# Strided x transposed by DMA instead of by TensorE, from the fifth batch on

## Chip, cores and metric

The kernel runs on one core of a Trainium2 chip. The metric is the device time of one launch in microseconds. One launch is profiled as well, and the views below come from that execution. TensorE is called PE, VectorE DVE, ScalarE ACT, GpSimd POOL and SyncE SP, as in the profile.

## What is computed

Sparse attention, and a two-layer network with an ELU on its output:

```
# q, k, v: (8 batches, 8 heads, 576 rows, 64)
rel  = pos[:, None] - pos[None, :]
local   = (rel >= 0) & (rel < 32)                    # heads 0 to 3
strided = (rel >= 0) & (key % 32 == query % 32)      # heads 4 to 7
attn = softmax(where(mask, q @ k.T / 8, -1e9)); y = attn @ v
x = y.transpose(0, 2, 1, 3).reshape(4608, 512)
h = x @ w_in                                         # 512 -> 2048
out = where(h > 0, h, exp(min(h, 0)) - 1) @ w_out    # 2048 -> 512
```

## The kernel before

**Attention.** Heads are taken in pairs, two local pairs (l0, l1) and two strided pairs (s0, s1) for each batch, all in bf16. For strided heads rows are regrouped by their remainder modulo 32, so that each of five groups of 108 or 126 rows needs only keys of the same group. q and k come from HBM in their natural layout, rows on partitions, into a ring of three tiles for each kind (`nat`), by software DMA that POOL issues (L191 to L219). From batch 3 on they are transposed to features on partitions by DMA transposes that SP issues (`transpose_batch`, L222).

A pair then runs in pieces: scores on PE (`scores_all`, L466) into the two banks of `pair_a` and two single banks; exp on ACT and mask on DVE; two value products on PE (`av`, L552), each followed on DVE by a reciprocal and the division into the tile x (L579, L580); and `x_out` (L595), which brings x to features on partitions in `xT`. For local pairs from batch 4 on, `x_out` is a DMA transpose from x right into `xT` (L599). For strided pairs PE transposes five groups into a PSUM bank (L607), and ACT copies them into `xT` in the order of the rows (L614, L616), since the groups interleave.

**MLP.** Tokens go in nine chunks of 512. In chunk nb, slot s = 0 to 15 issues one group of four matmuls of the first product (`moe_in`, L664; operands c = 0 to 3 of `xT`, of which c = 2 and 3 are the strided pairs s0 and s1), its ELU (`moe_act`, ACT L690, DVE L697 and L699) and one group of four of the second product (`moe_out`, L713). Every fourth such group ends an output block of 128 rows: ACT copies it to `o_sb` (L718) and SP stores it (L720).

**Order.** Nothing is scheduled by a planner: the program order on each engine is written out. While chunk nb runs, batch nb + 1 goes through attention, its pieces hung into half-slots: half-slot 2s comes ahead of `moe_in` of slot s, 2s + 1 behind it. A row of `TIMES` gives the half-slot where each of the four pairs begins and `PIECES` the offsets of its pieces. From batch 4 on local pairs come first. The first group of chunk nb + 1 needs the columns of batch nb + 1, so `x_out` of the last pair, at half-slot 31, is close to its reader.

SP's queue holds, in program order, the stores, the DMA transposes of q and k of batch nb + 2 and those of x; each waits at the head of the queue for its inputs. PSUM banks are handed out in rings; in these chunks two single banks (`ring`) serve the scores' last blocks, the value products and the strided transposes in turn.

The pieces of batch 4 and later, before:

```
PIECES = (-2, -1, 0, 2, 3, 5, 7, 0)
((2, 8, 15, 22), 0, PIECES)     # where the four pairs begin
# scores at +0, value products at +3 and +5 (+4 for the first pair)
(at[6] + (b > 1 and pr.strided) + (b >= LATE), pr.x_out)
```

Of the kernel before, what the change touches and what calls it, by code (L numbers as in the profile page):

```python
# [14 lines left out]
ACT = mybir.ActivationFunctionType  # L15
# [14 lines left out]
C_ORDER = (2, 3, 0, 1)  # L30


PIECES = (-2, -1, 0, 2, 3, 5, 7, 0)
TIMES = (
    None,
    None,
    ((4, 10, 15, 21), 0, (-3, -2, 0, 2, 4, 6, 9, 2)),
    ((2, 9, 15, 22), 0, (-2, -1, 0, 2, 3, 5, 8, 0)),
    ((2, 8, 15, 22), 0, PIECES),
)  # L40


# [23 lines left out]
def kernel(  # L66
# [66 lines left out]
    def bf16_bank():  # L133
        return rings["ring"].next().bitcast(BF16)
# [17 lines left out]
    def several(n, name, *shape):  # L152
        return [consts.tile([128, *shape], BF16, tag=f"{name}{i}", name=f"{name}{i}")
                for i in range(n)]

    nat = {(n, kind): several(3, f"{n}_{kind}", w * D)
           for n in "qk" for kind, w in (("str", 20), ("loc", 4 * L_RUN))}

# [10 lines left out]
    BY_DMA = 3  # L171

    WHOLE = 2

    FAR = 1
    RAW = 1
# [42 lines left out]
                out=t[0:64, a, 4],  # L219
                in_=src[name][b, 2 * a:2 * a + 2, 512:576].rearrange("h p d -> p h d"))  # L220

    def transpose_batch(b, local):  # L222

        def strided():
            for name, to in (("q", qT), ("k", kT)):
                nc.sync.dma_start_transpose(out=to["str"][b % 2],
                                            in_=nat[name, "str"][b % 3])

        if BY_DMA <= b <= LATE and local < 2:
            strided()  # L230
        if b >= EARLY and local:
            for name, to, o in (("q", qT, 0), ("k", kT, 32)):
                for a in range(2):
                    nc.sync.dma_start_transpose(
                        out=to["loc"][b % 2][:, a, o:o + 640].rearrange(
                            "p (i r) -> p i r", r=128),
                        in_=nat[name, "loc"][b % 3][:, 640 * a:640 * a + 640])
        if b > LATE:
            strided()

    def load_batch(b):
        for name in "qkv":
# [9 lines left out]
    def clear_nat(i, names="kq", heads=slice(0, 4)):  # L252

        for name in names:
            t = nat[name, "str"][i].rearrange("p (h x) -> p h x", h=4)
            nc.vector.memset(t[96:128, heads], 0.0)
# [6 lines left out]
    def clear_v(i, engine=nc.vector):  # L263
# [8 lines left out]
             for n in "q"}  # L272
# [2 lines left out]
    nc.scalar.activation(warm, ones[0:1, 0:1], ACT.Exp)  # L275
    nc.scalar.activation(rden.rearrange("p b s h r g -> p (b s h r g)"),
                         ones.to_broadcast([128, B * 48]), ACT.Copy)
    clear_nat(0)
    for i in range(2):
        nc.vector.memset(kT["str"][i][:, :, 126:128], 0.0)  # L280
# [70 lines left out]
    class Pair:  # L351
# [200 lines left out]
        def av(self, u):  # L552
            blocks = self.blocks(u)
            nk, nq = blocks[0][4:]
            b0 = blocks[0][1]
            n = len(blocks) // 2
            av = rings["ring"].next()[:, 0:6 * (D + 1)].rearrange(
                "q (p g d) -> q p g d", p=2, g=3)
            apart = self.strided and self.b == RAW
            vt = raw[RAW] if apart else (v_str if self.strided else v_loc)[self.b % 3]  # L560
            for p, blk, bank, i, _, _ in blocks:

                if self.b >= WHOLE:
                    pr, o, top = self.pr_all, self.probs[p, blk], 1152
                else:
                    pr, o, top = self.pr[u], (bank * n + i) * nq, 2 * n * nq
                m = 128 if o + 128 <= top else nq
                to = av[0:m, p, blk - b0, :]
                nc.tensor.matmul(to[:, 0:D] if apart else to, lhsT=pr[0:nk, o:o + m],  # L569
                                 rhs=vt[0:nk, 2 * self.hp + p, blk, :],  # L570
                                 start=True, stop=True)
                if apart:
                    nc.tensor.matmul(to[:, D:], lhsT=pr[0:nk, o:o + m],
                                     rhs=ones[0:nk, :], start=True, stop=True)
            if self.x is None:
                self.x = p_x.tile([128, 6, 2, D], BF16, tag=f"x_{self.kind}",
                                  name=f"x_{self.kind}")
            r = rden[0:nq, self.b, int(self.strided), self.hp, :, b0:b0 + n]
            nc.vector.reciprocal(r, av[0:nq, :, 0:n, D])  # L579
            nc.vector.tensor_tensor(  # L580
                self.x[0:nq, b0:b0 + n].rearrange("q g p d -> q p g d"),
                av[0:nq, :, 0:n, 0:D],
                r.unsqueeze(3).to_broadcast([nq, 2, n, D]),
                op=ALU.mult)

        def step(self, what):
# [5 lines left out]
            else:  # L592
                getattr(self, {"x": "x_out"}.get(what, what))()

        def x_out(self):  # L595
            c = 2 * int(self.strided) + self.hp
            dst = xT[:, c, self.b * S:(self.b + 1) * S]
            if self.b >= LATE and not self.strided:
                nc.sync.dma_start_transpose(  # L599
                    out=dst.rearrange("d (i q) -> d i q", i=6),  # L600
                    in_=self.x[0:LB].rearrange("q i p d -> q (i p d)"))
                return
            xt = bf16_bank()
            if self.strided:
                for g in range(5):
                    n = G_ROWS[g]
                    nc.tensor.transpose(  # L607
                        xt[:, 126 * g:126 * g + n],
                        self.x[0:n, g].rearrange("q p d -> q (p d)"),
                        identity[0:n, 0:n])  # L610
                rows = dst.rearrange("d (t r) -> d t r", r=STRIDE)
                groups = xt[:, 0:630].rearrange("d (g q) -> d g q", g=5)
                copy = self.copy("x", False)
                copy(rows[:, :, 0:30].rearrange("d t (r g) -> d t r g", g=5),  # L614
                     groups[:, :, 0:108].rearrange("d g (t r) -> d t r g", r=6))
                copy(rows[:, :, 30:32],  # L616
                     groups[:, 0:2, 108:126].rearrange("d g t -> d t g"))
            else:
                for i in range(6):
                    nc.tensor.transpose(  # L620
                        xt[:, LB * i:LB * (i + 1)],
                        self.x[0:LB, i].rearrange("q p d -> q (p d)"),
                        identity[0:LB, 0:LB])
                self.copy("x", self.b > 1)(dst, xt[:, 0:S])
# [10 lines left out]
    def attention(b, start, pitch, at):  # L635

        gaps = {}
        pairs = [Pair(b, s, hp) for s in (b < LATE, b >= LATE) for hp in range(2)]
        begin = [start + pitch * i for i in range(4)] if pitch else start
        if b >= LATE:  # L640
            gaps[begin[0]] = [pairs[3].halo]
        for i, pr in enumerate(pairs):
            for off, piece in ((at[0], pr.t_q), (at[1], pr.t_k),
                               (at[7], lambda pr=pr: pr.v_in(0)),
                               (at[7] + (b > 1), lambda pr=pr: pr.v_in(1)),
                               (at[2], lambda pr=pr: pr.scores(0)),
                               (at[3] if b < WHOLE else at[2] + (b < LATE),
                                lambda pr=pr: pr.scores(1)),
                               (at[4], lambda pr=pr: pr.av(0)),
                               (at[5] - (b >= LATE and i == 0),  # L650
                                lambda pr=pr: pr.av(1)),
                               (at[6] + (b > 1 and pr.strided) + (b >= LATE), pr.x_out), (at[5] - 2, pr.halo if b < LATE else lambda: None)):
                gaps.setdefault(begin[i] + off, []).append(piece)
        return gaps


# [145 lines left out]
    for nb in range(n_chunks + 1):  # L802
# [14 lines left out]
        for s in range(MC):  # L817
            if nb == 0 and s == 11:
                share([pair_a], b_halves, singles[3:], singles[:3])
            if s == (9 if nb + 2 > LATE else 6) and nb > 0 and nb + 2 < B:  # L820
                transpose_batch(nb + 2, int(nb + 2 >= LATE))
            if s == 13 and nb + 2 == EARLY:
                transpose_batch(nb + 2, 2)
            run(gaps, (2 * s,) if s else range(-10, 1))
            late = LATE <= nb + 1 and s + 1 < MC
            if nb < n_chunks:
                moe_in(nb, s)
            if nb < n_chunks and not late:
                moe_act(nb, s)
            run(gaps, (2 * s + 1,) if s + 1 < MC else range(2 * s + 1, 1000))  # L830
            if nb < n_chunks and late:
                moe_act(nb, s)
            if nb == B and s == 4:
                range_flag(row_ok16)
            for chunk, i in outs(nb, s):
                moe_out(chunk, i)
# [165 lines left out]
```

## Time and profile before

| | |
|---|---|
| Runs | 321.51, 318.53, 321.12 us (median 321.12) |
| Profiled execution | 318.57 us, span 316.8 us |
| Busy in the span | PE 95%, DVE 77%, ACT 55%, POOL 43% |
| Mean granted PE clock | 0.996 |
| DMA | 36.33 MB, mean 115 GB/s |
| Strided transposes of x on PE (L607) | 80, of which 40 in batches 4 to 7 |
| DMA transposes issued by SP | 10 + 10 local q and k, 5 + 5 strided q and k, 8 local x |

In the page a group is a line, engine, operation and tiles, with its count, busy time and mean. In the timeline the first column is the start in us from the start of the span, the second the length; a bracket gives the idle time ahead of the instruction and what ended it. The busy time of PE is modelled, and matmuls overlap. PEld is the loading of weights. SPq is SP's instruction queue: its DMA rows are the time of issuing, and the time to landing stands in the DMA issue rows.

### The profile page before, as it was taken

How to read it: one execution, taken by the hardware profiler on the slowest of the kernel's cores; microseconds unless marked ns; L12 is line 12 of the kernel's file. 1: busy time of each engine (PE TensorE's matmuls, PEld its weight loads, DVE VectorE, ACT ScalarE, POOL GpSimd, SP SyncE). 2: the span in 40 equal slices, each digit the busy share in tenths (PEclk: the TensorE clock that was granted, in tenths of full speed). 3: DMA queues.
4: the chain of work that ended last, by engine and by line, in shares of the span. 5: the costliest groups of instructions: out<-in, count | busy, mean ns of one | idle time of the engine just before them, and what ended most of it. 6: DMA issues, size and time to landing. Idle time of an engine off the chain costs nothing.

```text
span 316.8 us, 6114 instructions
## 1 busy us (share of the span) xinstructions
PE 299.8 (95%) x2240; PEld 149.1 (47%) x2240; DVE 242.6 (77%) x544; ACT 172.9 (55%) x335; POOL 137.5 (43%) x213
## 2 busy tenths in 40 slices
PE   1778989999999999999999999999999999999994
PEld 0454545545444554445444544454445444444443
DVE  7787797887889998987898788878897666766610
ACT  3577886777355645565546555655565444343411
POOL 9859526959959859958585810000000000000000
PEclk9999999999999999999999999999999999999998
DMA  6999999999999999999999992580210000101012
GB/s 108 163 179 157 167 207 126 156 124 183 139 125 167 157 187 138 99 163 154 177 163 117 163 175 61 88 156 35 68 35 35 34 33 35 66 34 36 33 68 73
DMA packets 108970, 36.33 MB, mean 115 GB/s; under 512 B 87357, under 2 KB 104453, under 8 KB 108933
## 3 DMA queue, kind: packets, MB, share of 16 engines
q0 software_dynamic: 71632, 18.10, 65.0%
q1 hardware_dynamic: 37301, 17.77, 29.1%
q8 instruction: 19, 0.31, 0.4%
q14 instruction: 18, 0.15, 0.1%
HBM read 36.70 MB, written 9.44 MB: 146 GB/s over the span
## 4 chain that ended last, share of the span: by engine, by line
PE 84%; DMA 6%; DVE 3%; POOL 2%; ACT 2%; issue 1%; POOLq 0%; ACTq 0%
PE single L713 39%; PE half L664 28%; PE single L664 9%; PE single L569 3%; DMA q_str<-in_q_dram 3%; PE pair_a L479 2%; DMA v_raw<-in_v_dram 2%; DMA k_str<-in_k_dram 2%; PE single L607 1%; ACT e_sb L690 1%; POOL k_str L191 1%; PE single L397 1%; DVE g_sb L699 1%; PE single L383 1%; DVE x_l L580 1%
## 5 line engine op out<-in xcount | busy, mean ns | idle before, releaser
L713 PE MATMUL single<-w_out_sb,g_sb 128*128 128x512 bf16 (+1 forms) x592 | 145.9, 373 | 0.0
L664 PE MATMUL half<-xT,w_in_sb 128*128 128x512 bf16 x436 | 112.6, 379 | 0.9 <-DVE g_sb L699 0.9
L690 ACT ACTIVATE e_sb<-half 128x512 f32<-128x512 f32 x109 | 65.3, 600 | 70.9 <-PE half L664 67.9
L697 DVE TENSOR_SCALAR e_sb<-e_sb 128x512 bf16<-128x512 f32 x140 | 62.5, 446 | 34.9 <-ACT e_sb L690 34.4
L713 PEld LDWEIGHTS <-g_sb 128*128 128x128 bf16 x592 | 54.8, 98 | 56.6
L664 PEld LDWEIGHTS <-w_in_sb 128*128 128x128 bf16 x576 | 52.4, 98 | 57.0 <-issue 1.3
L699 DVE TENSOR_TENSOR g_sb<-e_sb,half 128x512 bf16<-128x512 bf16 x106 | 72.9, 688 | 3.7
L664 PE MATMUL single<-xT,w_in_sb 128*128 128x512 bf16 x140 | 36.5, 379 | 0.0
L690 ACT ACTIVATE e_sb<-single 128x512 f32<-128x512 f32 x35 | 21.1, 602 | 24.4 <-PE single L664 22.3
L718 ACT COPY o_sb<-single 128x512 f32<-128x512 f32 (+1 forms) x37 | 21.2, 574 | 17.5 <-PE single L713 16.7
L485 ACT ACTIVATE pr<-pair_a 126x936 bf16<-126x936 f32 (+1 forms) x24 | 23.1, 961 | 12.4 <-PE single L479 11.9
L569 PEld LDWEIGHTS <-pr 128*128 128x128 bf16 (+3 forms) x352 | 20.0, 101 | 13.7 <-issue 1.3
L699 DVE TENSOR_TENSOR g_sb<-e_sb,single 128x512 bf16<-128x512 bf16 x34 | 23.4, 688 | 1.2
L191 POOL DMA_DIRECT2D k_str<-in_k_dram x32 | 21.1, 698 | 6.8 <-issue 2.6
L191 POOL DMA_DIRECT2D v_raw<-in_v_dram x32 | 20.7, 683 | 5.0 <-DVE v_str L436 3.7
L191 POOL DMA_DIRECT2D q_str<-in_q_dram x28 | 17.4, 641 | 4.1 <-DMA w_out_sb<-in_moe_w_out_dram 2.3
L580 DVE TENSOR_TENSOR x_l<-single,rden 96x384 bf16<-96x384 f32 x32 | 17.7, 554 | 1.1
L580 DVE TENSOR_TENSOR x_s<-single,rden 126x256 bf16<-126x256 f32 (+1 forms) x32 | 15.7, 491 | 1.1
L214 POOL DMA_DIRECT2D k_loc<-in_k_dram x20 | 15.3, 795 | 2.5 <-issue 1.5
L214 POOL DMA_DIRECT2D q_loc<-in_q_dram x20 | 15.8, 813 | 0.7 <-DMA k_str<-in_k_dram 0.7
L579 DVE RECIPROCAL rden<-single 96x6 f32<-96x6 f32 (+2 forms) x64 | 11.8, 185 | 2.0 <-PE single L569 1.6
L569 PE MATMUL single<-v_loc,pr 128*128 128x65 bf16 x192 | 11.6, 195 | 0.8 <-ACT v_loc L444 0.3
(115 smaller groups left out, 249.6 us busy)
## 6 DMA issues: line engine op xcount, KB each, us to landing
out_dram<-o_sb SPq DMA_DIRECT2D x35, 256.0 KB, 3.6
v_loc<-in_v_dram POOLq DMA_DIRECT2D x8, 288.0 KB, 8.2
k_str<-in_k_dram POOLq DMA_DIRECT2D x32, 67.5 KB, 5.0
v_raw<-in_v_dram POOLq DMA_DIRECT2D x32, 67.5 KB, 4.8
w_in_sb<-in_moe_w_in_dram POOLq DMA_DIRECT2D x4, 512.0 KB, 8.2
w_out_sb<-in_moe_w_out_dram POOLq DMA_DIRECT2D x4, 512.0 KB, 13.6
q_str<-in_q_dram POOLq DMA_DIRECT2D x28, 67.5 KB, 7.5
q_loc<-in_q_dram POOLq DMA_DIRECT2D x20, 64.0 KB, 5.2
```

The costliest lines, as they stand in the source:

```text
L191: engine.dma_start(out=t[0:108, h].rearrange("p g d -> p (g d)"), in_=rows[h, :, 0:30, :].rearrange("t (r g) d -> t r (g d)", g=5))
L214: nc.gpsimd.dma_start(out=t[:, h // 2, 0:4, h % 2], in_=src[name][b, h, 0:512].rearrange("(i p) d -> p i d", p=128))
L485: nc.scalar.activation(both, sc[0:nk, :, 0:w], ACT.Exp, scale=scale)
L569: nc.tensor.matmul(to[:, 0:D] if apart else to, lhsT=pr[0:nk, o:o + m], rhs=vt[0:nk, 2 * self.hp + p, blk, :], start=True, stop=True)
L579: nc.vector.reciprocal(r, av[0:nq, :, 0:n, D])
L580: nc.vector.tensor_tensor(self.x[0:nq, b0:b0 + n].rearrange("q g p d -> q p g d"), av[0:nq, :, 0:n, 0:D], r.unsqueeze(3).to_broadcast([nq, ...
L664: nc.tensor.matmul(hps, lhsT=w_in_sb[:, c, m * 128:(m + 1) * 128], rhs=xT[:, c, nb * N_TILE:(nb + 1) * N_TILE], start=start, stop=stop)
L690: nc.scalar.activation(e_sb, hps, ACT.Exp)
L697: nc.vector.tensor_scalar(e1_sb, e_sb, scalar1=1.0, scalar2=1.0, op0=ALU.min, op1=ALU.subtract)
L699: nc.vector.tensor_tensor(g_of[nb][:, m, :], e1_sb, hps, op=ALU.max)
L713: nc.tensor.matmul(ops, lhsT=g_of[nb][:, m, kk * 128:(kk + 1) * 128], rhs=w_out_sb[:, m, cols], start=(m == 0), stop=(m == MC - 1))
L718: nc.scalar.copy(o_sb, ops)
```

## The change

From batch 4 on (`X_DMA`), the x of a strided pair is transposed by a DMA that SP issues, one half-slot after the second value product. It goes into the free part of the pair's own q tile (the strided q of that batch, already transposed), 640 of its 1280 columns for each pair. `x_out` copies from there on ACT; PE takes no part and no PSUM bank is used. `x_out` comes three half-slots later relative to the pair's beginning (`X_WAIT`), but never behind half-slot 31. The strided pairs begin at half-slots 14 and 20 instead of 15 and 22, so that s1's `x_out` stays at 31, s0's moves from 24 to 26, and the DMAs are issued at half-slots 20 and 26.

x of strided pairs lies in two tiles of its own, for all batches, whose last 32 partitions are set once at the start by two ACT instructions. `TURNS` spreads the transposes of q and k: for batches 5 and later local ones at slot 8, strided q at 11 and strided k at 14 (all six at slot 9 before); for batch 4 all at slot 6 as before, but local ones first.

```diff
+TURNS = ((13, 6, 6), (6, 6, 6), (8, 11, 14))
-    ((2, 8, 15, 22), 0, PIECES),
+    ((2, 8, 14, 20), 0, PIECES),
...
+    x_str = several(2, "x_s", 6, 2, D)
+    X_DMA = 4
+    X_ONE = LATE
+    X_WAIT = 3
...
-    def transpose_batch(b, local):
-        ...
+    def transpose_batch(b, s):
+        for what, at in zip(("loc", "str q", "str k"), TURNS[min(b - EARLY, 2)]):
+            if s != at:
+                continue
+            if what == "loc":
+                ...                       # four local transposes, as before
+            else:
+                name = what[-1]
+                nc.sync.dma_start_transpose(out=(qT if name == "q" else kT)["str"][b % 2],
                                             in_=nat[name, "str"][b % 3])
...
+    for i in range(2):
+        nc.scalar.activation(x_str[i][96:128].rearrange("q g p d -> q (g p d)"),
+                             ones[96:128].to_broadcast([32, 12 * D]), ACT.Copy)
...
-            if self.x is None:
+            if self.strided:
+                self.x = x_str[self.hp]
+            elif self.x is None:
...
+        def by_dma(self):
+            if self.strided:
+                return self.b >= X_DMA
+            return self.b >= LATE or self.b >= X_ONE and self.hp == 0
+        def x_dma(self):
+            if self.strided and self.by_dma():
+                free = nat["q", "str"][self.b % 3][:, 640 * self.hp:640 * self.hp + 640]
+                self.x_t = free.rearrange("d (g q) -> d g q", g=5)
+                nc.sync.dma_start_transpose(
+                    out=self.x_t,
+                    in_=self.x[:, 0:5].rearrange("q g p d -> q (g p d)"))
...
-            xt = bf16_bank()
+            if not self.by_dma():
+                xt = bf16_bank()
             if self.strided:
-                (five PE transposes; groups = xt ...)
+                if self.by_dma():
+                    groups = self.x_t
+                else:
+                    (five PE transposes; groups = xt ..., as before)
                 copy = self.copy("x", False)
...
-                               (at[6] + (b > 1 and pr.strided) + (b >= LATE), pr.x_out), ...):
-                gaps.setdefault(begin[i] + off, []).append(piece)
+                               (at[5] + 1, pr.x_dma),
+                               (at[6] + (b > 1 and pr.strided) + (b >= LATE)
+                                + X_WAIT * (pr.strided and pr.by_dma()), pr.x_out), ...):
+                gaps.setdefault(min(begin[i] + off, 31), []).append(piece)
...
-            if s == (9 if nb + 2 > LATE else 6) and nb > 0 and nb + 2 < B:
-                transpose_batch(nb + 2, int(nb + 2 >= LATE))
-            if s == 13 and nb + 2 == EARLY:
-                transpose_batch(nb + 2, 2)
+            if nb > 0 and nb + 2 < B:
+                if s in TURNS[min(nb + 2 - EARLY, 2)]:
+                    transpose_batch(nb + 2, s)
```

More of the change, by code (lines that the diff above doesn't have):

```diff
@@ L220, in load_local @@
                 in_=src[name][b, 2 * a:2 * a + 2, 512:576].rearrange("h p d -> p h d"))
-    def transpose_batch(b, local):
-        def strided():
-            for name, to in (("q", qT), ("k", kT)):
-                nc.sync.dma_start_transpose(out=to["str"][b % 2],
-                                            in_=nat[name, "str"][b % 3])
[L229 to L239, printed above, removed]
+    def transpose_batch(b, s):
[3 more added lines that the diff above has]
+            if what == "loc":
+                for name, to, o in (("q", qT, 0), ("k", kT, 32)):
+                    for a in range(2):
+                        nc.sync.dma_start_transpose(
+                            out=to["loc"][b % 2][:, a, o:o + 640].rearrange(
+                                "p (i r) -> p i r", r=128),
+                            in_=nat[name, "loc"][b % 3][:, 640 * a:640 * a + 640])
+            else:
+                name = what[-1]
+                nc.sync.dma_start_transpose(out=(qT if name == "q" else kT)["str"][b % 2],
+                                            in_=nat[name, "str"][b % 3])
     def load_batch(b):
@@ L593, in step @@
                 getattr(self, {"x": "x_out"}.get(what, what))()
+        def by_dma(self):
[6 more added lines that the diff above has]
+                self.x_t = free.rearrange("d (g q) -> d g q", g=5)
+                nc.sync.dma_start_transpose(
+                    out=self.x_t,
+                    in_=self.x[:, 0:5].rearrange("q g p d -> q (g p d)"))
         def x_out(self):
@@ L597, in x_out @@
             dst = xT[:, c, self.b * S:(self.b + 1) * S]
-            if self.b >= LATE and not self.strided:
+            if self.by_dma() and not self.strided:
                 nc.sync.dma_start_transpose(
@@ L602, in x_out @@
                 return
-            xt = bf16_bank()
+            if not self.by_dma():
+                xt = bf16_bank()
             if self.strided:
[L605 to L610, printed above, removed]
-                rows = dst.rearrange("d (t r) -> d t r", r=STRIDE)
-                groups = xt[:, 0:630].rearrange("d (g q) -> d g q", g=5)
+                rows = dst.rearrange("d (t r) -> d t r", r=STRIDE)
+                if self.by_dma():
+                    groups = self.x_t
+                else:
+                    for g in range(5):
+                        n = G_ROWS[g]
+                        nc.tensor.transpose(
+                            xt[:, 126 * g:126 * g + n],
+                            self.x[0:n, g].rearrange("q p d -> q (p d)"),
+                            identity[0:n, 0:n])
+                    groups = xt[:, 0:630].rearrange("d (g q) -> d g q", g=5)
                 copy = self.copy("x", False)
@@ L651, in attention @@
                                 lambda pr=pr: pr.av(1)),
-                               (at[6] + (b > 1 and pr.strided) + (b >= LATE), pr.x_out), (at[5] - 2, pr.halo if b < LATE else lambda: None)):
-                gaps.setdefault(begin[i] + off, []).append(piece)
+                               (at[5] + 1, pr.x_dma),
+                               (at[6] + (b > 1 and pr.strided) + (b >= LATE)
+                                + X_WAIT * (pr.strided and pr.by_dma()), pr.x_out), (at[5] - 2, pr.halo if b < LATE else lambda: None)):
+                gaps.setdefault(min(begin[i] + off, 31), []).append(piece)
         return gaps
```

## The prediction

> **What bounds the kernel now.** I read the page first: the engine totals and the chain that ended last.
>
> ```profile
> span 316.8 us, 6114 instructions
> PE 299.8 (95%) x2240; PEld 149.1 (47%) x2240; DVE 242.6 (77%) x544; ACT 172.9 (55%) x335; POOL 137.5 (43%) x213
> ...
> PE 84%; DMA 6%; DVE 3%; POOL 2%; ACT 2%; issue 1%; POOLq 0%; ACTq 0%
> ```
>
> TensorE is busy for 95% of the span and carries 84% of the chain. The average hides the stages, so I cut the span where a chunk of the first MLP product begins (the first L664 group after the pair of strided transposes). The windows are the four chunks, 3 to 6, in which batches 4 to 7 are worked on. The columns are window, length, then busy time and count of PE, PEld, DVE, ACT and POOL, granted clock, DMA share and GB/s.
>
> ```profile
> 119.46:150.74 31.28, 31.28 (x226) 15.14 (x225) 27.26 (x60) 17.41 (x35) 26.26 (x39) 1.00 1.55 137
> 150.74:182.41 31.67, 31.64 (x227) 15.22 (x226) 27.10 (x60) 17.78 (x37) 22.27 (x33) 1.00 1.56 155
> 182.41:213.86 31.45, 31.45 (x227) 15.23 (x226) 26.49 (x60) 17.67 (x37) 1.20 (x1) 1.00 0.77 120
> 213.86:245.00 31.14, 31.14 (x226) 15.14 (x225) 26.20 (x59) 17.36 (x37) 0.00 (x0) 1.00 0.15 44
> ```
>
> PE has no gap in any of them, at full clock. So a PE instruction that is taken out shortens the chunk by its own issue time, and a PE wait that is put in lengthens it by its whole length: nothing later gives it back. The last two columns make a second distinction: in chunks 3 and 4 the DMA engines are oversubscribed (1.55 counts overlapping packets), in chunk 5 only partly, in chunk 6 hardly.
>
> **What is removed.** Eight strided outputs (two in each of the four batches) lose five PE transposes each. Here is the second half of chunk 4 on PE, with the value products (L569) that the next part uses:
>
> ```profile
> 170.53 0.37 PE L569 MATMUL single<-v_str,pr 108*128 108x65 bf16 x6
> ...
> 175.77 0.29 PE L569 MATMUL single<-v_str,pr 126*128 126x65 bf16 x4
> ...
> 181.29 0.42 PE L607 MATMUL single<-identity,x_s 126*128 126x126 bf16 x5
> 181.55 1.03 PE L713 MATMUL single<-w_out_sb,g_sb 128*128 128x512 bf16 x4
> 182.41 1.03 PE L664 MATMUL half<-xT,w_in_sb 128*128 128x512 bf16 x4
> ```
>
> Matmuls overlap, so the price of a set is not 0.42 but the distance to the next start: 181.55 - 181.29 = 0.26 us. Eight sets: **-2.1 us**. By their busy time it would be 8 x 0.42 = 3.4 us, which I keep as the upper bound. This already caps the gain: 2.1 of 318.6 is 0.7%, and one per cent, 3.2 us, is about what a measurement of this kernel can tell from no change.
>
> **What is added, and where it can wait.** The second strided pair of a batch (s1) is the critical one. Its transposed x is the fourth operand (c = 3) of the first L664 group of the next chunk. Today PE transposes it just before and ScalarE copies it in time. After the change SP issues a transpose of 128x640 after the pair's last division, and ScalarE copies from the landing place at the same point of its program as now. I place it in chunk 4:
>
> ```profile
> 163.69 0.36 PE L569 MATMUL single<-v_loc,pr 128*128 128x65 bf16 x6
> 164.31 0.55 DVE L580 TENSOR_TENSOR x_l<-single,rden 96x384 bf16<-96x384 f32 x1
> ...
> 176.97 0.58 ACT L718 COPY o_sb<-single 128x512 f32<-128x512 f32 x1 [0.33 <-PE single L713]
> 177.83 0.60 ACT L690 ACTIVATE e_sb<-half 128x512 f32<-128x512 f32 x1 [0.28 <-DVE g_sb L699]
> 179.77 0.60 ACT L690 ACTIVATE e_sb<-single 128x512 f32<-128x512 f32 x1 [1.34 <-PE single L664]
> ...
> 181.99 0.60 ACT L614 COPY xT<-single 128x540 bf16<-128x540 bf16 x1
> 182.48 0.21 ACT L616 COPY xT<-single 128x36 bf16<-128x36 bf16 x1
> ```
>
> With the pair two half-slots earlier, its second value product stands where the first stands now (175.77), less the 0.26 of the other pair's set: 175.51. A six-matmul product is divided 1.17 us after its start (164.31 + 0.55 - 163.69), so x is ready at 176.7. In SP's order the output store of that chunk comes first: its o_sb ends at 176.97 + 0.58 - 0.26, and 0.08 later for the longer value product, so at 177.4. SP's own rows give what follows:
>
> ```profile
> 162.15 3.94 SPq L599 DMA_TRANSPOSE xT<-x_l  x2
> 169.48 0.34 SPq L720 DMA_DIRECT2D out_dram<-o_sb  x1
> 170.00 2.74 SPq L234 DMA_TRANSPOSE qT_loc<-q_loc  x2
> 172.89 2.65 SPq L234 DMA_TRANSPOSE kT_loc<-k_loc  x2
> 175.64 3.07 SPq L226 DMA_TRANSPOSE qT_str<-q_str  x1
> 178.76 2.54 SPq L226 DMA_TRANSPOSE kT_str<-k_str  x1
> ```
>
> The store takes 0.34 and the step to the next transpose 0.18 (170.00 - 169.48 - 0.34), so the new transpose starts at about 177.9. The reader is at 182.41 less two sets (0.52) plus three of the group's four matmuls (0.65): 182.54. The copies need 0.70 (182.48 + 0.21 - 181.99) and about 0.1 of hand-over. So the **decisive number** is the landing time: up to 182.54 - 0.80 - 177.9 = 3.85 us nothing waits, beyond it PE waits one for one. The issue rows give the landing of transposes and stores (last figure, us from issue); the first two are x_l beside loads in chunk 4 and x_l in the quiet chunk 6, each just behind a store:
>
> ```profile
> xT<-x_l SPq DMA_TRANSPOSE x1, 5.6
> ...
> xT<-x_l SPq DMA_TRANSPOSE x2, 2.6
> ...
> out_dram<-o_sb SPq DMA_DIRECT2D x1, 256.0 KB, 3.9
> ...
> qT_loc<-q_loc SPq DMA_TRANSPOSE x1, 5.3
> ...
> qT_loc<-q_loc SPq DMA_TRANSPOSE x2, 3.7
> ...
> qT_str<-q_str SPq DMA_TRANSPOSE x1, 7.6
> ```
>
> The third is a store beside loads (chunk 4), the fourth a 128x640 transpose in chunk 3, the fifth the same shape in chunk 5, the sixth a transpose of twice the size in chunk 4. The nearest row for chunks 3 and 4 is x_l at 5.6: same place behind a store, similar size, same traffic. It gives 5.6 - 3.85 = 1.75 us of PE wait, twice: **+3.5 us**. For chunks 5 and 6 the landing of 2.6 to 3.7 is inside the slack: 0. Bounds for the busy chunks: 3.9, as the store, gives nothing (0.1); 7.6 gives 3.75 each, 7.5.
>
> **Other parts that I cost at nothing, with their cover.** The first strided pair (s0) is issued near 170.8 (its value product is one half-slot, 0.87, earlier than 170.5, plus 1.17), lands 5.6 later at 176.4, and is copied only after o_sb, at 177.4; at 7.6 ScalarE would wait 1.0 us, and it is idle 0.28 and 1.34 us ahead of its next activations there. SP: the four local transposes move ahead of the second local output and take 5.6 us (2.74 + 2.65 and gaps), so x_l of pair 1 is issued near 169 instead of 164.9; it is read at 182. The strided q transpose (3.07) then ends near 175.1, 2.3 us before SP needs to be free for the store. The k one follows behind the new transpose, near 179 to 182, and is read seven slots into the next chunk, some 13 us later.
>
> ```profile
> 2.15 0.50 ACT L276 ACTIVATE rden<-ones 128x384 f32<-128x384 bf16 x1
> 5.96 0.82 ACT L370 CAST q_str<-q_stage 126x256 bf16<-126x256 f32 x2 [3.30 <-DMA q_stage<-in_q_dram]
> ...
> 158.49 1.23 POOL L191 DMA_DIRECT2D q_str<-in_q_dram  x2
> 182.92 1.20 POOL L202 DMA_DIRECT2D v_loc<-in_v_dram  x1 [0.85 <-issue]
> ```
>
> The two initialising activations (32x768, at most twice the 0.50 of 384 elements each) fit into ScalarE's 3.30 us wait for q; uncovered, 2 us. The load of batch 7 into batch 4's q tile must now wait for a copy at the end of chunk 3, near 151; POOL reaches the load at 158.5, so 7 us cover a late copy. The added transfers in chunks 3 and 4 delay POOL's loads; the last is issued at 183, and SP first needs it near 195. The order for batch 4 (local before strided) delays strided transposes that are read a chunk later. Copying from SBUF instead of PSUM: the cast of L370 reads SBUF at 0.41 us a piece, 256 and 384 elements, no worse than 0.60 for 540.
>
> **Earlier pairs and the two shared PSUM banks.** Pairs 2 and 3 now issue scores only one half-slot after the last value product of the pair ahead, instead of two. The last two score matmuls need the bank that the division reads. Time from value product to them: 0.19 + 0.87 + 0.21 = 1.27 us, against 1.17 for the division: free, barely. It can miss; this is what a miss looks like in chunk 4 at a place with two half-slots:
>
> ```profile
> 158.60 0.39 PE L479 MATMUL pair_a<-qT_loc,kT_loc 64*128 64x96 bf16 x10
> 158.82 0.43 PE L479 MATMUL single<-qT_loc,kT_loc 64*128 64x96 bf16 x2
> 159.18 1.04 PE L664 MATMUL half<-xT,w_in_sb 128*128 128x512 bf16 x4
> ```
>
> The two take 0.36 to the next start where 0.14 is usual elsewhere, so 0.22 us. Eight such places cost between 0 and 1.8 us; I take **+0.3**, since the usual division clears it. Against this, two uses of the banks per chunk fall away, which I count as nothing.
>
> **Sum:** -2.1 + 3.5 + 0.3 = **+1.7 us** on the profiled execution's 318.57 us (span 316.8 and 1.8 around it). The runs shown are 321.51, 318.53 and 321.12, median 321.12: the profiled one lies with the lowest. I set the base midway, at 319.8, and forecast 321.5 us.
>
> **Rivals.**
> (a) *The transposes land in time everywhere.* For: 3.7 and 2.6 without loads, and the clump of six transposes that fills SP from 170.0 to 181.3 is now spread. Against: 5.3 to 7.6 beside loads. Then -2.1 + 0.3 = -1.8: 318.0 us. The Trainium skill's page "DMA: Bandwidth & Descriptors", section "Latency and other measured facts", gives a transpose 261 GB/s; by that figure 164 KB would be, as an estimate, 0.6 us behind the issue, and this rival would hold. The rows of 5.6 and 2.6 speak against so short a time.
> (b) *The strided transposes pile up on the queue.* Place: SP's new order puts q (1280 columns), a store, and then x in a row, and the x copy is behind all. Price: with the 7.6 of the q transpose, 3.75 us in each busy chunk, and with 4.1 instead of 3.7 at most 0.3 in each quiet one: -2.1 + 7.5 + 0.3 + 0.5 = +6.2: 326.0 us, slower. It decides once the landing in chunks 3 and 4 passes 6.6 us (2.75 us each, which gives +3.7). For: the DMA share of 1.56 in that window. Against: fewer transposes in flight than now.
> (c) *The gain goes into bank waits.* Landing in time, but all eight early scores miss: -2.1 + 1.8 = -0.3: 319.5 us. For: margin 0.1 us. Against: it clears by the usual row.
>
> **How the numbers follow.** Forecast 0.45 (its own range, landing 4.3 to 6.6: 318.9 to 323.5), (a) 0.27, (b) 0.20, (c) 0.08. The range takes the middle of (a) and of (b) in, with the spread of the base: 317.5 to 326.0. Faster by over 1% needs 3.2 us, above the cap of 2.1; only the busy-time bound reaches it: 0.06. Slower by over 1% is (b) and the top of the forecast: 0.28. Within 1%: 0.66.
>
> **What would show it.** Right: no L607 groups after chunk 2 on PE; in chunks 3 and 4 an idle time of PE at the fourth L664 matmul of the next chunk, released by ScalarE's x copy, and that copy waiting for the DMA transpose; none in chunks 5 and 6; chunk 6 at 30.6 us. Wrong: chunks 3 and 4 also near 30.8 (then the landing was below 3.9), a wait of chunk 6, PE idle at the L479 singles in more than two places, or time lost outside these four chunks.

## Result and the profile after

The changed kernel is slower: 329.30 us against 320.79 us (medians of six runs each), a ratio of 1.0264 with a 95% interval of 1.0207 to 1.0321. The forecast was 321.5 us, its range 317.5 to 326.0. The profiled execution took 328.94 us, its span is 327.1 us, 10.3 us longer than before.

Line numbers have moved: L695 is the first product (L664 before) and L744 the second (L713), L721 and L730 are the first and the last step of the ELU (L690, L699), L592 is the division into x, L616 the new transpose, L643 and L645 the copies of x into `xT` (L614, L616 before), and L239 and L245 the transposes of local and strided q and k.

The page, engine totals and chain:

```profile
span 327.1 us, 6031 instructions
PE 297.7 (91%) x2161; PEld 147.3 (45%) x2200; DVE 242.8 (74%) x544; ACT 178.4 (55%) x337; POOL 136.2 (42%) x213
...
PE 69%; DMA 13%; DVE 6%; POOL 4%; issue 3%; ACT 2%; SPq 1%; ACTq 0%; DVEq 0%; POOLq 0%
```

TensorE has lost its hold on the chain: 84% became 69%, and DMA rose from 6% to 13%. The windows of PE alone, cut at the same places (first L695 group of chunks 3 to 7; columns: window, length, busy PE, granted clock, DMA share, GB/s):

```profile
118.94:153.84 34.90, 31.43 (x216) 1.00 1.55 169
153.84:189.38 35.54, 32.71 (x212) 0.90 1.48 143
189.38:223.24 33.86, 30.78 (x213) 1.00 0.73 114
223.24:254.77 31.53, 30.89 (x213) 1.00 0.34 56
```

Lengths before were 31.28, 31.67, 31.45 and about 31.5. The wait of a chunk's fourth matmul falls behind the cut, so into the next window; I therefore read the ends of the chunks. The waits by engine, and PE around the end of chunk 3 and of chunk 4:

```profile
ACT xT L643 <- DMA q_str<-x_s: 10.2, 4, 4.5
...
PE half L695 <- ACT xT L645: 6.0, 3, 2.8
```

```profile
149.71 1.03 PE L744 MATMUL single<-w_out_sb,g_sb 128*128 128x512 bf16 x4
153.84 1.32 PE L695 MATMUL half<-xT,w_in_sb 128*128 128x512 bf16 x3 [3.10 <-DMA qT_str<-q_str]
157.68 0.58 PE L695 MATMUL half<-xT,w_in_sb 128*128 128x512 bf16 x1 [2.51 <-ACT xT L645]
158.06 1.91 PE L744 MATMUL single<-w_out_sb,g_sb 128*128 128x512 bf16 x4
159.90 0.58 PE L489 MATMUL pair_a<-qT_loc,kT_loc 64*128 64x96 bf16 x10
...
192.96 0.38 PE L695 MATMUL half<-xT,w_in_sb 128*128 128x512 bf16 x1 [2.77 <-ACT xT L645]
```

The fourth L695 matmul waits for ScalarE's copy of x, as forecast: it starts 3.8 us after the first three at the end of chunk 3, where 0.65 is usual (3.2 lost), and 3.6 us after them at the end of chunk 4 (189.38 to 192.96, 2.9 lost). But at the end of chunk 3 PE also stood still a group earlier: from 149.71 to 153.84, 4.1 us for a group of 0.86. The profile puts that to a DMA that is not its input; ScalarE and VectorE show what it was:

```profile
150.63 1.10 ACT L643 COPY xT<-q_str 128x540 bf16<-128x540 bf16 x1 [4.45 <-DMA q_str<-x_s]
...
153.10 0.69 DVE L730 TENSOR_TENSOR g_sb<-e_sb,half 128x512 bf16<-128x512 bf16 x1
...
156.40 1.10 ACT L643 COPY xT<-q_str 128x540 bf16<-128x540 bf16 x1 [3.07 <-DMA q_str<-x_s]
...
191.68 1.10 ACT L643 COPY xT<-q_str 128x540 bf16<-128x540 bf16 x1 [2.37 <-DMA q_str<-x_s]
```

ScalarE stood 4.45 us at the head of its queue for s0's x. Three exponentials of the first MLP product queued behind it, so three PSUM banks stayed full and PE had none for the next group: VectorE's last read of one (L730) ends at 153.79, and PE starts at 153.84. And the copy itself takes 1.10 us instead of 0.60. SP's queue in chunk 3:

```profile
137.09 4.92 SPq L239 DMA_TRANSPOSE kT_loc<-k_loc  x2
142.12 1.33 SPq L624 DMA_TRANSPOSE xT<-x_l  x1
143.96 0.34 SPq L751 DMA_DIRECT2D out_dram<-o_sb  x1
144.42 1.31 SPq L616 DMA_TRANSPOSE q_str<-x_s  x1
145.77 3.13 SPq L245 DMA_TRANSPOSE qT_str<-q_str  x1
149.01 0.52 SPq L751 DMA_DIRECT2D out_dram<-o_sb  x1
149.63 1.29 SPq L616 DMA_TRANSPOSE q_str<-x_s  x1
```

The second x was divided at 145.52 (144.96 + 0.56 on DVE) and issued at 149.63: SP was still with what came before. It landed 6.67 us later. The first x, divided at 139.54 (138.98 + 0.56), was issued at 144.42, 4.9 us late, for the same reason. The four local transposes hold SP from 133.36 to 142.01, 8.65 us, where those of chunk 4 take 5.30 (171.06 to 176.36). They were not waiting for their own loads: POOL issued these at 98.9 to 106.2, and they landed within 4.2 us.

The chain that ended last shows which of the two waits set the end of chunk 3:

```profile
145.77 3.13 SPq L245
...
149.63 6.67 DMA q_str<-x_s
...
156.40 0.07 ACT xT L643
...
157.68 0.58 PE half L695
```

It runs over SP and the landing of s1's x; s0's copy is not on it. By this chain, had PE not stood still behind 149.71, its fourth matmul would have waited for s1's copy all the same. So the two losses at this end, 3.3 and 3.2 us, are one delay of 6.5 us, and s0's wait is a second, smaller limit behind it (experiment 6 brings it out).

Last, the granted clock of PE after this pause:

```profile
153.80:157.70 3.90, 1.35 (x4) 0.52 1.70 198
...
158.10:160.00 1.90, 1.90 (x9) 0.50 4.27 122
160.00:162.00 2.00, 2.00 (x19) 0.80 2.87 115
162.00:166.00 4.00, 3.94 (x30) 1.00 1.14 155
```

The clock fell to half near 154.0, with the first three matmuls, and came back near 160.8, some 3 us after the fourth. That stretched the group at 158.06 to 1.84 us up to the next start instead of 0.96, the scores by 0.2 and the next group by 0.2: about 1.4 us with what lies between (158.06 to 161.51, against 151.61 to 153.80 before, and 0.17 ahead of it).

The sum by starts: 3.3 + 3.2 + 1.4 at the end of chunk 3, 2.9, 0.5 and 0.9 at the ends of chunks 4, 5 and 6, together 12.2 us, less the 2.1 us of removed transposes: 10.1 of the span's 10.3 us.

### The profile page after: what moved, and what is told of

Read it like the earlier page. It is cut to its first block, busy times and chain, and to the rows that moved or that the text cites. A ratio compares the mean times of both kernels' runs of the same rounds, so it can differ in the third digit from the quotient of the medians.

```text
span 327.1 us, 6031 instructions
## 1 busy us (share of the span) xinstructions
PE 297.7 (91%) x2161; PEld 147.3 (45%) x2200; DVE 242.8 (74%) x544; ACT 178.4 (55%) x337; POOL 136.2 (42%) x213
## 4 chain that ended last, share of the span: by engine, by line
PE 69%; DMA 13%; DVE 6%; POOL 4%; issue 3%; ACT 2%; SPq 1%; ACTq 0%; DVEq 0%; POOLq 0%
PE single L744 33%; PE half L695 23%; PE single L695 7%; DMA q_str<-x_s 5%; DMA w_out_sb<-in_moe_w_out_dram 5%; PE single L579 3%; PE pair_a L489 2%; DVE g_sb L730 2%; DMA v_raw<-in_v_dram 2%; DVE e_sb L728 1%; DVE x_s L592 1%; SPq L245 1%; DMA k_str<-in_k_dram 1%; POOL k_str L200 1%; POOL w_out_sb L813 1%
## 5 line engine op out<-in xcount | busy, mean ns | idle before, releaser
L744 PE MATMUL single<-w_out_sb,g_sb 128*128 128x512 bf16 (+1 forms) x579 | 144.6, 375 | 1.0 <-issue 0.3
L695 PE MATMUL half<-xT,w_in_sb 128*128 128x512 bf16 x419 | 111.0, 382 | 11.3 <-ACT xT L645 6.0
L721 ACT ACTIVATE e_sb<-half 128x512 f32<-128x512 f32 x109 | 65.1, 599 | 68.5 <-PE half L695 61.5
L744 PEld LDWEIGHTS <-g_sb 128*128 128x128 bf16 x592 | 55.0, 98 | 64.0 <-issue 8.5
L695 PEld LDWEIGHTS <-w_in_sb 128*128 128x128 bf16 x576 | 52.9, 98 | 62.6 <-issue 5.1
L730 DVE TENSOR_TENSOR g_sb<-e_sb,half 128x512 bf16<-128x512 bf16 x106 | 72.9, 688 | 3.9
L695 PE MATMUL single<-xT,w_in_sb 128*128 128x512 bf16 x133 | 35.8, 379 | 0.7 <-ACT xT L645 0.3
L721 ACT ACTIVATE e_sb<-single 128x512 f32<-128x512 f32 x35 | 21.1, 602 | 23.8 <-PE single L695 22.4
L730 DVE TENSOR_TENSOR g_sb<-e_sb,single 128x512 bf16<-128x512 bf16 x34 | 23.4, 688 | 1.6 <-PE single L489 0.5
L200 POOL DMA_DIRECT2D v_raw<-in_v_dram x32 | 19.9, 649 | 10.9 <-DVE v_str L446 9.4
L200 POOL DMA_DIRECT2D k_str<-in_k_dram x32 | 19.8, 639 | 8.1 <-issue 2.9
L592 DVE TENSOR_TENSOR x_l<-single,rden 96x384 bf16<-96x384 f32 x32 | 17.7, 554 | 1.1
L592 DVE TENSOR_TENSOR x_s<-single,rden 126x256 bf16<-126x256 f32 (+1 forms) x32 | 15.7, 491 | 1.1
L643 ACT COPY xT<-q_str 128x540 bf16<-128x540 bf16 x8 | 8.9, 1112 | 11.4 <-DMA q_str<-x_s 10.2
```

The costliest lines, as they stand in the source:

```text
L200: engine.dma_start(out=t[0:108, h].rearrange("p g d -> p (g d)"), in_=rows[h, :, 0:30, :].rearrange("t (r g) d -> t r (g d)", g=5))
L592: nc.vector.tensor_tensor(self.x[0:nq, b0:b0 + n].rearrange("q g p d -> q p g d"), av[0:nq, :, 0:n, 0:D], r.unsqueeze(3).to_broadcast([nq, ...
L695: nc.tensor.matmul(hps, lhsT=w_in_sb[:, c, m * 128:(m + 1) * 128], rhs=xT[:, c, nb * N_TILE:(nb + 1) * N_TILE], start=start, stop=stop)
L721: nc.scalar.activation(e_sb, hps, ACT.Exp)
L730: nc.vector.tensor_tensor(g_of[nb][:, m, :], e1_sb, hps, op=ALU.max)
L744: nc.tensor.matmul(ops, lhsT=g_of[nb][:, m, kk * 128:(kk + 1) * 128], rhs=w_out_sb[:, m, cols], start=(m == 0), stop=(m == MC - 1))
```

## Experiments

Every edit is against the changed kernel, ratios are against the kernel before.

**1. No strided x by DMA, all else kept.**

```diff
-    X_DMA = 4
+    X_DMA = 8
```

> The changed kernel with PE transposes for all strided x again (X_DMA = 8): the earlier pairs, the new slots of the q and k transposes and the two x tiles of their own stay. Theory A (the time is lost where ScalarE waits for the landing of the x transposes): as the kernel before, 319 to 322 us, no PE idle over 1 us in chunks 3 to 6. Rival B (earlier pairs and the new slots of the q and k transposes cost it, through PSUM banks or late q and k): most of the 8.5 us stays, 326 us or more.

Measured: 320.12 us, ratio 0.9995 (0.9956 to 1.0034). No PE start is late by over 0.35 us between 100 and 245 us. Rival B has fallen: earlier pairs, the new slots of the q and k transposes and the fixed x tiles cost nothing that shows. The loss needs x to go by DMA. (With it the copy's delay of three half-slots goes too, since it hangs on the same switch.)

**2. Strided x by DMA in the quiet chunks only.**

```diff
-    X_DMA = 4
+    X_DMA = 6
```

> Strided x by DMA in batches 6 and 7 alone (X_DMA = 6), whose x is transposed in chunks 5 and 6, with few or no loads beside it. Theory A: the ends of chunks 3 and 4 (8.0 and 2.9 us of PE idle in the changed kernel) are gone, those of 5 and 6 stay at 0.3 and 0.9, and 1.0 us of PE work is saved: 320 to 322 us. Rival C (the slower copy out of SBUF, 1.11 us for 0.60, loads ScalarE): half of the loss stays, about 325 us.

Measured: 319.42 us, ratio 0.9997 (0.9955 to 1.0039). The losses in chunks 3 and 4 are gone. The two waits at the fourth L695 matmul are 0.5 us each, as large as what two removed sets save in a chunk (0.52): the change gives nothing even where the landing is quick.

**3. The first strided pair alone.**

```diff
-                return self.b >= X_DMA
+                return self.b >= X_DMA and self.hp == 0
```

> Strided x by DMA for the first strided pair alone, in all four batches; the second goes through PE again. Theory A in its form 'ScalarE stands still for s0 too': in chunk 3 ScalarE still waits about 4 us for s0's landing at half-slot 26, and PE loses about 3 us behind it, in chunk 4 about 1 us or nothing; no wait of the fourth L695 matmul on the x copy anywhere: 321 to 324 us. Rival D (only the last pair's landing matters, s0 has slack): under 321 us, no PE idle over 1 us in chunk 3.

Measured: 322.23 us, ratio 1.0048 (0.9997 to 1.0098), not clearly different. ScalarE waited once for over 1 us:

```profile
151.34 1.12 ACT L643 COPY xT<-q_str 128x540 bf16<-128x540 bf16 x1 [1.25 <-DMA q_loc<-in_q_dram]
```

The time lies in theory A's range, but its mechanism, 4 us of waiting and 3 of PE idle, did not show; rival D's sign, no PE idle over 1 us, did. The reason: the start of the program to the first scores of chunk 3 took 3.2 us more in this execution (124.30 against 121.11 us), so the loads stood elsewhere relative to the transposes, and no PE start in the chunks was late by over 0.35 us. The first x was issued 1.2 us after its division there (143.44 to 144.60), not 4.9. The first pair alone does little harm; whether it costs half a per cent stays open, since that difference lies ahead of chunk 3 in the profile.

**4. The second strided pair alone.**

```diff
-                return self.b >= X_DMA
+                return self.b >= X_DMA and self.hp == 1
```

> Strided x by DMA for the second strided pair alone, in all four batches; the first goes through PE. Theory A: ScalarE no longer stands still at half-slot 26, so the 3.3 us of PE idle ahead of the last groups of chunk 3 are gone; the waits at the fourth L695 matmul stay at 2 to 3 us in chunks 3 and 4 and 0.5 to 0.9 in 5 and 6: 323 to 325 us. Rival K (the two pairs' losses add up, s0 alone cost 1.5 us): 327 us.

Measured: 324.88 us, ratio 1.0111 (1.0047 to 1.0175), inside the 323 to 325 expected of theory A. PE at the end of chunk 3 and its clock there:

```profile
151.18 0.81 PE L695 MATMUL half<-xT,w_in_sb 128*128 128x512 bf16 x3
156.68 0.59 PE L695 MATMUL half<-xT,w_in_sb 128*128 128x512 bf16 x1 [4.69 <-ACT xT L645]
```

```profile
153.00:157.00 4.00, 0.32 (x1) 0.69 1.60 141
157.00:161.00 4.00, 4.00 (x21) 0.50 3.42 122
```

The wait of the last pair alone is 4.7 us there, against 2 to 3 expected, and it brings the half clock with it; at the end of chunk 4 the loss is 0.9, against 2 to 3 expected. So the time came out inside the range partly by luck. The x of chunk 3 was issued at 147.26, 0.9 us after its division, and ScalarE, idle for 4.3 us, began its copy only 8.1 us after the issue. So without s0's transpose on SP, and without the late issue, a long landing made most of this loss. The profiled execution was the longest of the four (326.86 us). The two pairs alone cost 0.5% and 1.1%, together 2.6%. With both, s0's transpose stands on SP ahead of the q transpose and of s1's x (144.42 to 145.73 above), but what makes the whole larger than the sum is not shown.

**5. Without the loads of batches 6 and 7.**

```diff
-        if nb + 3 < B:
+        if nb + 3 < 6:
             load_batch(nb + 3)
+        elif nb + 3 < B:
+            raw[nb + 3] = raw[nb + 1]
```

> The changed kernel without the loads of batches 6 and 7 (these batches compute on what lies in the tiles), so that POOL's loads end in chunk 3, before the x transposes. Theory A in its form 'loads beside the transposes make the landing late': x transposes land within 2.6 to 4.2 us in all chunks, ScalarE's waits for them fall from 10.2 us to under 2, 319 to 322 us. Rival E (SP's own order makes it late: q and k transposes and stores ahead of x): the waits in chunks 3 and 4 keep at least half of their length, 324 us or more.

Measured: 319.98 us, ratio 1.0006 (0.9965 to 1.0048). The kernel leaves these loads out and computes on what lies in the tiles. Its profiled execution was the longest of its ten (323.83 us), so only single lengths are read from it. Issue and landing of the x transposes, first in the changed kernel, then here (minimum, median, maximum; ns for the issue, us for the landing):

```profile
L616 SPq DMA_TRANSPOSE q_str<-x_s x8: 1213/1272/2107, 144.4 to 250.8; - x8
...
DMA to landing us min/median/max: 2.6/4.6/6.7
```

```profile
L616 SPq DMA_TRANSPOSE q_str<-x_s x8: 1212/1248/1255, 146.2 to 245.7; - x8
...
DMA to landing us min/median/max: 2.6/2.6/2.6
```

The landings are not those of all eight: in the changed kernel the trace gives two, 6.7 in chunk 3 and 2.6 in chunk 5, and here it gives 2.6 in both chunks. The first strided q transpose on SP behind the first x is shorter too (1.4 us in place of 3.1), and the four local ones ahead of it take 5.3 in place of 8.7. So the loads are needed for the loss: they stretch both the landing and SP's own work ahead of it. What is left is 0.5 us at the ends of chunks 3 to 5 and 0.8 at that of 6, together about the 2.1 us saved.

**6. SP's order: x ahead of the strided q transpose.**

```diff
-TURNS = ((13, 6, 6), (6, 6, 6), (8, 11, 14))
+TURNS = ((13, 6, 6), (6, 6, 6), (8, 14, 14))
```

> The changed kernel with the strided q transposes of batches 5 and later moved from slot 11 to slot 14, so that SP holds only a store between the two x transposes. In the changed kernel the last x of chunk 3 was divided at 145.5 us and issued at 149.6, behind s0's x and the q transpose. Theory F (SP's order adds to the landing time): the issue in chunk 3 comes 2 to 3 us earlier, PE's wait at the fourth L695 matmul there falls by as much, 326 to 327.5 us. Theory A alone (the transfers wait for the loads, whatever SP's order): the landing lengthens instead, no change, 328.5 to 330 us.

Measured: 323.90 us, ratio 1.0128 (1.0078 to 1.0178): half of the loss is gone, more than expected. SP in chunk 3, then the copy and PE:

```profile
144.59 1.28 SPq L616 DMA_TRANSPOSE q_str<-x_s  x1
148.10 0.34 SPq L751 DMA_DIRECT2D out_dram<-o_sb  x1
148.53 1.25 SPq L616 DMA_TRANSPOSE q_str<-x_s  x1
149.83 2.75 SPq L245 DMA_TRANSPOSE qT_str<-q_str  x1
```

```profile
151.10 1.13 ACT L643 COPY xT<-q_str 128x540 bf16<-128x540 bf16 x1 [3.03 <-DMA q_loc<-in_q_dram]
...
153.79 1.13 ACT L643 COPY xT<-q_str 128x540 bf16<-128x540 bf16 x1
```

```profile
155.10 0.38 PE L695 MATMUL half<-xT,w_in_sb 128*128 128x512 bf16 x1 [0.16 <-ACT xT L645]
```

The chunk starts 1.7 us later in this execution, so the issue of the last x is 2.7 us earlier relative to it, and its copy starts 5.3 us after the issue without a wait. At the end of chunk 3 PE loses 2.6 us in place of 7.9 (3.3 + 3.2 + 1.4), now behind s0's copy (3.03; the profile names another DMA, but the copy reads only s0's x), and its clock stays at 1.00. Theory F holds, but order is not all: the landing, at most 5.3 us, was shorter as well, and the half clock went too, which the expected range had not counted. The prediction's rival (b) had the place right.

**7. The copy's order of dimensions turned.**

```diff
-  copy(rows[:, :, 0:30].rearrange("d t (r g) -> d t r g", g=5),
-       groups[:, :, 0:108].rearrange("d g (t r) -> d t r g", r=6))
+  copy(rows[:, :, 0:30].rearrange("d t (r g) -> d g t r", g=5),      # by DMA only
+       groups[:, :, 0:108].rearrange("d g (t r) -> d g t r", r=6))
```

> The changed kernel with the order of dimensions turned in the large copy of x by ScalarE: it reads a group's 108 columns one after the other and writes every fifth row, instead of reading one column of each group in turn. Theory G (the copy takes 1.11 us in place of 0.61 because it reads SBUF 256 bytes apart for each element): 0.6 to 0.7 us, and 0.4 to 0.5 us off each of the four chunk ends, 327 to 328 us. Rival H (any read of SBUF by ScalarE costs that): it stays near 1.1 us, 329 us.

Measured: 331.15 us, ratio 1.0334 (1.0277 to 1.0390); the copy took 1.79 us. Both theories missed. The same edit with `X_DMA = 6`, and with the first pair alone and its copy at half-slot 30 (`X_WAIT = 7`):

> Strided x by DMA in batches 6 and 7 alone, with the turned copy. Theory A with G: in chunks 5 and 6 nothing waits, the two waits of 0.5 us of the kernel with the unturned copy are gone, 1.0 us of PE work is saved: 318.5 to 319 us against 319.8, a ratio of 0.996 to 0.998. Rival H: as with the unturned copy, ratio 1.000.

> Strided x by DMA for the first strided pair alone, in all four batches, its copy at half-slot 30 instead of 26 and with the turned order; the second pair goes through PE. Theory A: a landing of 6 us is over by then, ScalarE waits nowhere for a transpose, four sets of PE transposes (1.0 us) are saved: ratio 0.996 to 0.998. Rival I (a landing of 6 us is not all, the added transposes also slow what shares SP or the DMA engines): ratio 1.000 or more, with waits for q, k or loads that the kernel before does not have.

Measured: 321.25 us, ratio 1.0052 (1.0015 to 1.0088), with waits of 1.05 us at the ends of chunks 5 and 6; and 321.64 us, 1.0058 (1.0025 to 1.0091). In the second no copy waited for a transpose, so theory A's part held; but the 1.8 us copy stands behind the other pair's copy just ahead of the next chunk, and PE starts there are late by 0.5 to 1.0 us.

**8. Four forms of the copy in one kernel, by batch.**

```diff
+  form = {2: "gather", 3: "scatter", 5: "gather", 6: "scatter", 7: "plain"}.get(self.b, "both")
```

> The changed kernel with four forms of the large copy of x, by batch, to see what makes it slow: batches 0, 1 (from PSUM) and 4 (from SBUF) as in the changed kernel; batches 2 (PSUM) and 5 (SBUF) read one column of each group in turn but write one after the other; 3 (PSUM) and 6 (SBUF) read one after the other and write every fifth row; 7 (SBUF) reads and writes one after the other. The rows of batches 2, 5 and 7 are left in the wrong order. Theory G2 (reading SBUF with 256 bytes between elements costs about 0.5 us, writing every fifth row costs about 1.2 us by itself): batch 5 at 1.1, batch 6 at 1.8, batch 7 at 0.6, batch 2 at 0.6, batch 3 at 1.8. Rival J (only SBUF as source is slow with any break in the order): batches 2 and 3 both at 0.6, batch 5 at 1.1, 6 at 1.8.

Measured: one execution, 332.56 us, from which only the lengths of the copies are read.

Groups by line and form (count, then busy us, mean ns). L653 writes every fifth row, L647 and L650 read one column of each group in turn and write rows as in the changed kernel (L647) or one after the other (L650), L656 does neither; the source is PSUM (single) or SBUF (q_str):

```profile
L653 ACT COPY xT<-q_str 128x540 bf16<-128x540 bf16 x2 | 3.6, 1792 | 0.0
L653 ACT COPY xT<-single 128x540 bf16<-128x540 bf16 x2 | 3.6, 1778 | 0.0
L647 ACT COPY xT<-single 128x540 bf16<-128x540 bf16 x4 | 2.4, 609 | 0.4 <-PE single L637 0.2
L650 ACT COPY xT<-q_str 128x540 bf16<-128x540 bf16 x2 | 2.2, 1107 | 2.4 <-DMA q_str<-x_s 1.7 <-DMA q_loc<-in_q_dram 0.7
L647 ACT COPY xT<-q_str 128x540 bf16<-128x540 bf16 x2 | 2.2, 1100 | 7.2 <-DMA q_str<-x_s 7.2
...
L656 ACT COPY xT<-q_str 128x540 bf16<-128x540 bf16 x2 | 1.3, 643 | 0.4 <-DMA q_str<-x_s 0.4
L650 ACT COPY xT<-single 128x540 bf16<-128x540 bf16 x2 | 1.2, 609 | 1.0 <-PE single L637 1.0
```

Theory G2 holds in every form. Read in a row, SBUF takes 643 ns; reading with 252 bytes between elements from PSUM takes no longer (609), while 256 bytes between them in SBUF cost 0.46 us (1100 and 1107); writing every fifth 2-byte row costs 1.2 us from either. The Trainium skill's page "SBUF — State Buffer", section "Door 1: The DMA port swizzle", says that successive accesses run at full speed only within the same 16-byte line. The SBUF reads agree with it. The writes, 10 bytes apart, cost more than reads 256 bytes apart, which it does not tell.

**9. DMA in the quiet chunks, the last copy one activation earlier.**

```diff
-    X_DMA = 4
+    X_DMA = 6
-                gaps.setdefault(min(begin[i] + off, 31), []).append(piece)
+                gaps.setdefault(min(begin[i] + off, 30), []).append(piece)
```

> Strided x by DMA in batches 6 and 7 alone, the copy of the last pair at half-slot 30 instead of 31, so one activation earlier on ScalarE. Theory A: the two waits of 0.5 us fall to 0 in chunk 5 and under 0.5 in chunk 6, up to 1.0 us saved, ratio 0.996 to 0.999. Rival L (the activation that now stands behind the copy delays the next group's second product by as much): ratio 1.000.

Measured: 319.31 us against 320.21, ratio 0.9964 (0.9930 to 0.9997). The copy of the last pair in chunk 5:

```profile
211.13 1.12 ACT L643 COPY xT<-q_str 128x540 bf16<-128x540 bf16 x1 [0.55 <-DMA q_str<-x_s]
```

It waits 0.55 us for the landing, and no PE instruction waits for it any more. This version is ahead of both kernels, by about the 1.0 us of four removed sets; the interval only just leaves 1 out.

## Why the prediction was wrong, point by point

- *What bounds the kernel, and what is removed: right.* PE waits came out one for one, and no set of PE transposes of strided x is left in these chunks; 12.2 - 2.1 makes up the change.
- *Where it waits: right.* The fourth L664 matmul of the next chunk waits for the copy, the copy for the transpose, most in chunks 3 and 4. The size was off: 6.5 and 2.9 us for 1.75 each, together 9.4 for the +3.5 of the sum.
- *The clock of SP: the step that failed most.* I worked out the issue of x in chunk 4 and took it for chunk 3 as well. In chunk 4 it came true: the last x was issued 1.1 us after its division, where I had 1.2. In chunk 3 I had, counted from the start of the chunk, s0's x at 20.1 us and s1's at 27.2; they were issued at 25.5 and 30.7. SP's issuing was slower there, 8.65 us for the local transposes where I had 5.6, and the q transpose, the store and both x stood behind it. Experiments 5 and 6 show both halves of it: without loads the four take 5.3, and with x ahead of q half of the loss goes.
- *Its other terms.* The landing of 5.6 was 6.7 in chunk 3 and 6.2, by the start of the copy, in chunk 4; in chunk 3 of experiment 4 it was up to 8.1, and there it, more than SP, made the loss. The copy was taken at its old 0.60, "no worse" than a cast from SBUF; but that cast reads in a row. It takes 1.10 and lies wholly between landing and reader. In the quiet chunks, where I had 0, it brought 0.5 in each, with 0.35 more of waiting for the landing in chunk 6, and it cancels the gain (experiments 2 and 5). With these sizes the sum works: chunk 4 gives 1.75 + 0.6 + 0.5 = 2.9, as measured, and chunk 3, with 3.5 us of late issue and 1.1 of landing, 1.75 + 3.5 + 1.1 + 0.5 = 6.9 against 6.5.
- *The first pair at no cost: wrong, but not what set the time.* I named the price of a late landing as 1.0 us of ScalarE's time, against idle time behind it. It was 4.45 us, most of it from the issue 4.9 us after the division, and I didn't ask what queues behind a waiting ScalarE: three exponentials, three PSUM banks, then PE. In the changed kernel s1's later copy covers it; once that is gone, it costs 2.6 us (experiment 6).
- *Bank waits of earlier pairs, +0.3: nothing shows* (experiment 1), and rival (c) falls with it. Two ACT instructions at the start, POOL's later load and the order for batch 4 cost nothing that shows.
- *Rivals.* (b), piling up on SP, had 0.20 and 326.0 us; experiment 6 shows that the order on SP carries half of the loss. Its price stood on a longer landing (7.6), though, and most of the excess in chunk 3 was late issue. (a) would have needed the quiet landing: with no loads the landing is 2.6, but the copy takes the gain.
- *Not in the forecast at all: the half clock* (next section but one). It cost 1.4 us; without it the time, 327.9 as an estimate, would still lie above the range.

## What to carry to other kernels

A transfer that takes the place of matmuls is paid by the time until its queue issues it, by its landing time beside the traffic of that stage, and by everything that its waiting reader holds up on its own queue. Work out the issuing queue in each stage with that stage's lengths, place the reader late enough for the slowest landing that the stage shows, and ask what queues behind it. Price a moved copy by its access pattern as well as its size: a pattern that is free from PSUM need not be free from SBUF. And put a latency-critical transfer ahead of those with slack on the queue that they share.

## What was new of the hardware

- After PE had stood still for 3.10 us (end of chunk 3) and for 4.69 us (experiment 4), its granted clock was 0.50 for some 4 us of work; after 2.77 us (end of chunk 4) it stayed at 1.00. The Trainium skill's page "TensorE: Matmul & The Clock Gate", section "What's actually happening", gives an idle window of about 3.4 us. These rows agree in size only: the pause of 3.10 us was shorter and sufficed, and in experiment 4 the clock fell some 2.5 us into the pause, by the profile's modelled ends of the matmuls.
- SP's own time for one strided q transpose in chunk 3 was 1.41 us without the loads of batches 6 and 7 (experiment 5) and 3.13 beside them; for the four local ones 5.3 and 8.65.
- ScalarE's copy of 540 two-byte elements: 0.61 to 0.64 us, 1.10 with a 256-byte step in SBUF reads, 1.79 with a 10-byte step in writes (experiment 8).
